# Decay rows issued from ScalarE, and token rows multiplied in two column groups after the value products

## The chip, the cores and the metric

The kernel runs on one core of one Trainium2 chip. The metric is the device time of one execution in microseconds; the kernel before takes 475.36 us (median of three runs, 474.98 to 475.89). The diagnosis rests on one profiled execution, which took 474.5 us.

## What is computed

Two blocks follow each other. The first is a recurrent gated linear attention over 4 batches, 8 heads, 768 tokens and a head dimension of 48. The second is a mixture of experts (8 experts, one per token, width 1024) over the resulting 3072 rows of 384.

```python
state = np.zeros((B, H, D, D))
for t in range(S):
    state = alpha[:, :, t, :, None] * state + np.einsum('bhd,bhde->bhde', k[:, :, t], v[:, :, t])
    y[:, :, t] = np.einsum('bhd,bhde->bhe', q[:, :, t], state)
x = y.transpose(0, 2, 1, 3).reshape(B * S, H * D)
logits = x @ w_gate
expert_idx = np.argmax(logits, axis=1)          # one expert per token
gate_w = softmax(logits)[expert_idx]
out = gate_w * (relu(x @ w1[expert]) @ w2[expert])
```

## The kernel before

**Tiling.** The tokens of a batch are cut into six chunks of 128. A *step* `s` is one chunk of one batch: chunk `c = s // 4`, batch `b = s % 4`, 24 steps in all. Within a chunk the recurrence is written as matrix products: with the cumulative product of the decays (`cp`, and its inverse `icp`), keys are multiplied by `icp` and queries by `cp` (`operands`, GpSimd), both are transposed on TensorE (`transposes`), their products give the scores (`scores`), which are masked (`mask`, VectorE, two tiles dA and dB) and multiplied with the values (`attend`). From the second chunk on, `read_state` adds the carried state, scaled by the decay over the chunk boundary (`scale_state`, the tile U). `keys_values` forms the state's increment. All three write one PSUM tile, `y`. Then `result` copies the outputs to SBUF as `yT` (ScalarE), `add_state` forms the new state (VectorE, the tile acc), `rows` turns `yT` into rows and router logits with one product per pair of heads (TensorE, the tile `x`), `logits` and `gate` make the router's weight (VectorE and ScalarE), and `keep_rows` writes the weighted rows `xs` to memory for the second block.

**Order of the work.** The order is written out by hand: a loop over `i` from -4 to 24 issues scores of step `i`, result and state of step `i-1`, transposes of `i+1`, operands of `i+2` and the exponentials of step `i+5` (lines 454 to 490). Each engine works through its own instructions in that order; waits between engines are put in by the framework. So on ScalarE an iteration runs: yT (line 367), logarithms (244), the copy of the keys kT (304), two exponentials (253, 254), the router's exponential gex (400), xs (408). On VectorE it runs: acc (375, 377), the masks dA and dB (319), the copy of the queries qT (302), at a chunk's end the decay rows er (269, 270), then lgn and lmin (393, 394) and gw (401, 402). On TensorE it runs: scores (311), at a chunk's start the turning of the decay rows ep (281), transposes (299), cum (250), x (383), the state's reading (338), attend (348), keys and values (359).

**The decay over a chunk boundary.** For each step one row of `cp` (the last) and one of `icp` (the first) are copied by DMA into a small tile `dec` (line 262). Once per chunk, `decay_rows` multiplies them with one row of alpha (the tile alpha0, loaded at line 264) into er, TensorE turns er into columns (`decay_cols`, ep), and VectorE copies these as E, which `scale_state` needs. ep and cum share one PSUM tile.

**SyncE's queue.** SyncE issues, in the loop's order, all loads of alpha, k, q and v (line 236, two steps at a time, some three iterations ahead), the decay rows (262), the alpha row (264), the weighted rows (409, which waits for xs), and from `i = 4` the first expert's weights (185, 188). ScalarE issues two small loads at the start and none in the loop.

**The second block.** After the loop a ranking of tokens (lines 498 to 622) is followed by gathers, the experts' products on TensorE and scatters (from line 829 on). None of it is touched; its first instruction waits for the last logits.

```python
            do(rows, i - 1)
            for s in sums[1:]:
                cums(s)
            do(read_state, i)
            do(attend, i)
            do(keys_values, i)
            do(logits, i - 1)
```

Of the kernel before, what the change touches and what calls it, by code (L numbers as in the profile page):

```python
# [18 lines left out]
def kernel(  # L19
# [26 lines left out]
    nc = tc.nc  # L46
    B, H, S, D = q.shape
    C = 128
    NB = S // C
# [4 lines left out]
    E = moe_w_gate.shape[1]  # L54
# [3 lines left out]
    D2 = 2 * D  # L58
    DP = 64
    HC = C // 2  # L60
# [18 lines left out]
    iw = consts.tile([C, NP, D2 + E], F32)  # L79
    alpha0 = consts.tile([B, NB, H, D], F32)  # L80
# [10 lines left out]
    def second_consts():  # L91
        nc.vector.tensor_scalar_mul(iw[:, :, D2:], iw[:, :, D2:], -1.0)
        for i in range(2):
            nc.vector.tensor_copy(
                iw[i * DP : (i + 1) * DP, :, i * D : (i + 1) * D],
                ident[i * DP : (i + 1) * DP, None, i * DP : i * DP + D].to_broadcast([DP, NP, D]),
            )
# [21 lines left out]
    def late_consts(i):  # L119
        if i == 0:  # L120
            nc.gpsimd.memset(lt_strict[:], 1.0)
            nc.gpsimd.affine_select(
                lt_strict[:], lt_strict[:], compare_op=ALU.is_gt, fill=0.0,
                base=0, pattern=[[1, C]], channel_multiplier=-1,
            )
            nc.gpsimd.memset(ones_sq[:], 1.0)
        if i == 1:
            nc.gpsimd.memset(zero_e[:], 0.0)
            nc.gpsimd.memset(keep[:], 1.0)
            nc.gpsimd.memset(keep[:, :, 0:1], 0.0)  # L130
        if i in (2, 3):
            for ti, tf, pattern, base, mult in list(iotas.values())[3 * (i - 2) : 3 * (i - 1)]:
                nc.gpsimd.iota(ti[:], pattern=pattern, base=base, channel_multiplier=mult)
                nc.gpsimd.tensor_copy(tf[:], ti[:])
            if i == 2:

                nc.gpsimd.memset(key0[:, 0:1], float(16 * N))
        if i == 4:

            nc.gpsimd.tensor_copy(iota_r[:], iota_f[:])  # L140
            nc.gpsimd.tensor_scalar(
                tok_n[:], tokv[:, NT // 2 :], scalar1=-1.0, scalar2=float(N // 2), op0=ALU.mult, op1=ALU.add,
            )
            nc.gpsimd.tensor_copy(tokv[:, NT // 2 :], tok_n[:])
# [33 lines left out]
    def fetch_part(g, i):  # L178

        if i == 0:  # L180
            g["w1"] = wpool.tile([C, DB, F], F32, name="w1")
            g["w2"] = wpool.tile([C, FB, Dm], F32, name="w2")
        if i < 6:
            a, h = i // 2, i % 2
            nc.sync.dma_start(g["w1"][:, a, h * F // 2 : (h + 1) * F // 2], moe_w1[0, a * C : (a + 1) * C, h * F // 2 : (h + 1) * F // 2])
        else:
            f = 2 * (i - 6)
            nc.sync.dma_start(
                g["w2"][:, f : f + 2], moe_w2[0, f * C : (f + 2) * C, :].rearrange("(a p) d -> p a d", p=C),
            )  # L190
# [24 lines left out]
    def cb(s):  # L215
        return s // B, s % B

    with tc.tile_pool(name="ld", bufs=6) as ld, \
# [6 lines left out]
        decay = {}  # L225
# [16 lines left out]
        def logs(s):  # L242
            t = work.tile([C, Dm], F32, name="lna", bufs=4)
            nc.scalar.activation(t[:], st[s]["a"].rearrange("s h d -> s (h d)"), AF.Ln)
            st[s]["lna"] = t

        def cums(s):
            c, b = cb(s)
            cum = ps.tile([C, 512], F32, name="cum")
            nc.tensor.matmul(cum[:, :Dm], lhsT=cum_m[:], rhs=st[s]["lna"][:], start=True, stop=True)  # L250
            cp = work.tile([C, Dm], F32, name="cp", bufs=6)
            icp = work.tile([C, Dm], F32, name="icp", bufs=6)
            nc.scalar.activation(icp[:], cum[:, :Dm], AF.Exp, scale=-1.0)
            nc.scalar.activation(cp[:], cum[:, :Dm], AF.Exp)
            st[s]["cp"], st[s]["icp"] = cp, icp


            for cc, i, row in ((c, 1, icp[0:1, :]), (c + 1, 0, cp[C - 1 :, :])):
                if 0 < cc < NB:
                    if cc not in decay:  # L260
                        decay[cc] = work.tile([B, 2, Dm], F32, name="dec", bufs=3)
                    nc.sync.dma_start(decay[cc][b : b + 1, i, :], row)
                if i and b == 0 and c:
                    nc.sync.dma_start(alpha0[:, c], alpha[:, :, c * C, :])

        def decay_rows(c):
            t = by_half(er[:B])
            d = decay[c].rearrange("b i (a p d) -> b i a p d", a=2, p=NP)
            nc.vector.tensor_tensor(t, d[:, 0], d[:, 1], op=ALU.mult)
            nc.vector.tensor_tensor(t, t, alpha0[:, c].rearrange("b (a p) d -> b a p d", a=2), op=ALU.mult)  # L270
# [7 lines left out]
        def decay_cols(c):  # L278
            ep = ps.tile([C, NP, C], F32, name="ep", tag="cum")
            for p in range(NP):  # L280
                nc.tensor.transpose(ep[:, p, :], pair(er[:], p), ident[:])
            decay[c] = work.tile([C, NP, B], F32, name="E", bufs=2)
            nc.vector.tensor_copy(decay[c][:], ep[:, :, :B])  # L283
# [95 lines left out]
        def rows(s):  # L379
            d = st[s]  # L380
            d["x"] = ps.tile([C, NP, C], F32, name="x")
            for m in range(NP):
                nc.tensor.matmul(  # L383
                    d["x"][:, m, : D2 + E], lhsT=d["yT"][:, m // 2, m % 2, :], rhs=iw[:, m, :], start=True, stop=True,
                )

        def at_row(s):
            c, b = cb(s)
# [23 lines left out]
        def do(f, i, *a):  # L412
            if 0 <= i < NT:
                f(i, *a)
# [7 lines left out]
        def new_sums(i):  # L422
            return range(sums_to(i - 1) + 1, sums_to(i) + 1)
# [10 lines left out]
        def loads_for(i):  # L434
            loads(("a", sums_to(i + 1)), ("v", i), ("k", i + 2), ("q", i + 2))

        def idle(n):

            t = ps.tile([C, NP, C], F32, name="sA")
            for _ in range(n):  # L440
                nc.tensor.matmul(t[:, :2, :], lhsT=er[:, 0].rearrange("s a d -> s (a d)"), rhs=er[:, :2], start=True, stop=True)
# [12 lines left out]
        for i in range(-4, NT + 1):  # L454
            loads_for(i + 3)
            do(scores, i)
            do(result, i - 1)
            do(add_state, i - 1)
            for s in new_sums(i + 1):
                logs(s)  # L460
            if 0 < i < NT and i % B == 0:
                decay_cols(i // B)
            do(mask, i, 0)
            do(mask, i, 1)
            if -2 < i < 0:
                idle(3)
            do(transposes, i + 1)
            sums = list(new_sums(i))
            for s in sums[:1]:
                cums(s)  # L470
            do(operands, i + 2)
            do(scale_state, i)
            if 0 < i + 1 < NT and (i + 1) % B == 0:
                decay_rows((i + 1) // B)
            do(rows, i - 1)
            for s in sums[1:]:
                cums(s)
            do(read_state, i)
            do(attend, i)
            do(keys_values, i)  # L480
            do(logits, i - 1)
            do(gate, i - 1)
            do(keep_rows, i - 1)
            if i == -3:
                second_consts()
            late_consts(i - 1)
            if 4 <= i < 14:
                fetch_part(groups[0], i - 4)
            if 15 <= i < 23:
                next(first_sums)  # L490
# [168 lines left out]
    def chain(g, terms, out, res):  # L659
# [44 lines left out]
        return p1, p2, p7, p6, p5, c22, p34  # L704

    def layer1(g, rows, ahead):
        n, m = g["n"], g["n"] // 2
        h0, h1 = slice(0, m), slice(m, n)
# [41 lines left out]
        for a in range(FH):  # L750
            p1, p2, p7, p6, p5, c22, p34 = tile_parts(a)
            p1()
            p2()
            p7()
            p6()
            if prev:
                prev()
            next(rows, None)
            p5()
            c22()  # L760
            prev = p34
# [175 lines left out]
```

## Time and profile before

| | |
|---|---|
| median of three runs | 475.36 us |
| the profiled execution | 474.5 us |
| its span on the core | 472.7 us |
| TensorE busy | 415.8 us (88%) |
| VectorE, ScalarE, GpSimd busy | 233.3, 171.8, 139.6 us |
| first block, to 171.5 us: TensorE busy | 147 us |
| ranking, 171.5 to 195 us: TensorE busy | 5.2 us |
| experts, from 195 us: TensorE busy | 263.7 us |
| DMA share, 69.7 to 125 us | 0.90, at 188 to 201 GB/s |
| granted clock of TensorE, 96.4 to 125 us | 0.88 |

A line of the timeline gives the start in us, the length in us, the engine, the source line, the operation, its output and inputs, shapes, and in brackets how long the engine was idle before it and which event ended that. PE is TensorE, PEld its loading of weights, DVE VectorE, ACT ScalarE, POOL GpSimd, SPq the queue of SyncE. A 32-bit product appears as two matmul instructions. Instructions in a row of one kind are merged ("x8").

### The profile page before, as it was taken

To read this page: it belongs to the slowest core of one execution; us is meant where nothing else is said; L and a number is where in the kernel's file an instruction comes from. 1 tells how busy PE (TensorE), PEld (TensorE's weight loads), DVE (VectorE), ACT (ScalarE), POOL (GpSimd) and SP (SyncE) were. 2 spreads that over 40 slices of the span, in tenths; PEclk is the share of its full clock that TensorE was granted. 3 is DMA by queue.
4 is the path that set the end of the run, shared out by engine and by line. 5 is a ranking of instruction groups with operands and counts; after the bars stand their busy time and mean duration, and the time that the engine had idled before them with its cause. 6 is when DMAs were issued, how large, how long until landed. Compare 5 with 4: busy or idle time off the path is not lost.

```text
span 472.7 us, 8960 instructions
## 1 busy us (share of the span) xinstructions
PE 415.8 (88%) x3356; PEld 362.7 (77%) x3356; DVE 233.3 (49%) x640; ACT 171.8 (36%) x454; POOL 139.6 (30%) x169
## 2 busy tenths in 40 slices
PE   7893979979799921699999999999999999999991
PEld 5683878868688811597997997997997988979970
DVE  3343534445556568347446447357257365473500
ACT  4652636446353410041352251251350431523511
POOL 3442432424567405710024024022041140200102
PEclk9997998979999965599999999999999999999997
DMA  9986788989862107414235225315414432400001
GB/s 178 203 175 129 162 198 177 185 197 218 185 138 68 53 33 266 123 41 133 61 124 190 91 96 187 128 57 187 150 44 174 168 118 91 172 2 17 31 0 49
DMA packets 119969, 59.05 MB, mean 125 GB/s; under 512 B 102806, under 2 KB 114159, under 8 KB 119924
## 3 DMA queue, kind: packets, MB, share of 16 engines
q1 hardware_dynamic: 116084, 48.86, 40.1%
q0 software_dynamic: 3424, 9.59, 5.8%
q8 instruction: 27, 0.44, 0.4%
q14 instruction: 18, 0.15, 0.1%
q10 hardware_dynamic: 416, 0.01, 0.0%
HBM read 48.95 MB, written 9.58 MB: 124 GB/s over the span
## 4 chain that ended last, share of the span: by engine, by line
PE 58%; issue 5%; DVE 4%; POOL 2%; ACT 1%; DMA 1%; POOLq 0%; ACTq 0%; DVEq 0%
PE pA L727 12%; PE pB L727 9%; PE pA L783 8%; PE pC L798 8%; PE pC L727 5%; PE pB L783 4%; PE pC L783 2%; PE tp L645 2%; PE sA L311 2%; PE y L348 1%; PE x L383 1%; PE tp L828 1%; PE tp L299 1%; PE y L338 1%; DVE xgT L646 1%
## 5 line engine op out<-in xcount | busy, mean ns | idle before, releaser
L815 POOL DMA_INDIRECT out_dram<-zo,s_idx x29 | 31.8, 1096 | 208.0 <-ACT zo L814 114.3
L671 ACT COPY u<-pA 128x212 f32<-128x212 f32 (+7 forms) x80 | 25.5, 318 | 83.5 <-PE pA L783 70.1
L173 DVE TENSOR_TENSOR h_sb<-pB,u 128x212 f32<-128x212 f32 (+7 forms) x64 | 23.1, 361 | 65.8 <-PE pB L727 49.2
L798 PE MATMUL pC<-h_sb,w 128*128 128x424 f32 (+7 forms) x128 | 43.9, 496 | 0.0
L289 POOL TENSOR_TENSOR kqb<-k_sb,icp 128x384 f32<-128x384 f32 x24 | 24.1, 1004 | 62.4 <-ACT xs L408 30.0
L798 PEld LDWEIGHTS pC<-h_sb,w 128*128 128x128 f32 x128 | 24.1, 190 | 16.0 <-issue 6.7
L727 PE MATMUL pA<-t,s 128*128 128x212 f32 (+7 forms) x128 | 33.2, 341 | 1.0 <-ACT u L671 0.4
L635 POOL DMA_INDIRECT xg<-x_rows,g_idx x29 | 30.0, 1033 | 10.7 <-issue 6.7
L727 PE MATMUL pA<-xgT,w 128*128 128x212 f32 (+7 forms) x128 | 32.5, 335 | 0.0
L383 PEld LDWEIGHTS x<-iw,yT 128*128 128x128 f32 x192 | 25.6, 197 | 6.9 <-ACT yT L367 1.4
L299 PE MATMUL tp<-ident,kqb 128*128 128x128 f32 x192 | 28.6, 294 | 1.3 <-POOL kqb L289 1.3
L176 DVE TENSOR_TENSOR th<-h_sb,th 128x212 f32<-128x212 f32 (+7 forms) x64 | 23.1, 361 | 10.5 <-ACT h_sb L740 10.5
L311 PE MATMUL sA<-qT,kT 48*128 48x128 f32 x192 | 27.7, 285 | 0.2 <-ACT kT L304 0.2
L671 ACT COPY p<-pA 128x212 f32<-128x212 f32 (+7 forms) x40 | 13.1, 328 | 40.4 <-DVE t L176 25.8
L311 PE MATMUL sB<-qT,kT 48*128 48x128 f32 x192 | 27.7, 285 | 0.0
L727 PE MATMUL pC<-xgT,w 128*128 128x212 f32 (+7 forms) x128 | 27.4, 338 | 0.0
L727 PE MATMUL pB<-t,w 128*128 128x212 f32 (+7 forms) x128 | 27.0, 333 | 0.0
L383 PE MATMUL x<-iw,yT 128*128 128x104 f32 x192 | 25.9, 280 | 1.1 <-ACT yT L367 1.1
L299 PEld LDWEIGHTS tp<-ident,kqb 128*128 128x128 f32 x192 | 22.7, 149 | 4.4 <-POOL kqb L289 2.3
L740 ACT ACTIVATE h_sb<-h_sb 128x424 f32<-128x424 f32 (+7 forms) x32 | 17.1, 533 | 24.0 <-DVE h_sb L173 24.0
L289 POOL TENSOR_TENSOR kqb<-q_sb,cp 128x384 f32<-128x384 f32 x24 | 24.9, 1035 | 2.3 <-DMA q_sb<-in_q_dram 2.3
L250 PE MATMUL cum<-lna,cum_m 128*128 128x384 f32 x48 | 21.7, 536 | 3.8 <-DVE E L283 2.5
(176 smaller groups left out, 930.7 us busy)
## 6 DMA issues: line engine op xcount, KB each, us to landing
w<-in_moe_w_dram SPq DMA_DIRECT2D x14, 1536.0 KB, 6.8
x_rows<-xs SPq DMA_DIRECT2D x24, 192.0 KB, 2.1
a_sb<-in_alpha_dram SPq DMA_DIRECT2D x11, 384.0 KB, 4.9
k_sb<-in_k_dram SPq DMA_DIRECT2D x11, 384.0 KB, 5.5
q_sb<-in_q_dram SPq DMA_DIRECT2D x11, 384.0 KB, 5.2
v_sb<-in_v_dram SPq DMA_DIRECT2D x11, 384.0 KB, 5.6
w<-in_moe_w_dram SPq DMA_DIRECT2D x6, 256.0 KB, 3.4
w<-in_moe_w_dram SPq DMA_DIRECT2D x4, 384.0 KB, 3.5
```

Source lines behind the costliest of these rows:

```text
L173: eng.tensor_tensor(out, a, b, op=ALU.add)
L176: eng.tensor_tensor(out, a, b, op=ALU.subtract)
L289: nc.gpsimd.tensor_tensor(by_half(kq[:, i]), d[n].rearrange("s (a p) d -> s a p d", a=2), d[e][:].rearrange("s (a p d) -> s a p d", a=2, p ...
L299: nc.tensor.transpose(tp[:, p, :], pair(kqb[s % 3][:, i], p), ident[:])
L311: nc.tensor.matmul(t[:, p, :], lhsT=d["kT"][r : r + D, p, :], rhs=d["qT"][r : r + D, p, :], start=True, stop=True,)
L383: nc.tensor.matmul(d["x"][:, m, : D2 + E], lhsT=d["yT"][:, m // 2, m % 2, :], rhs=iw[:, m, :], start=True, stop=True,)
L635: nc.gpsimd.indirect_dma_start(out=g["xg"][:r, j, :], out_offset=None, in_=x_d[:, :], in_offset=bass.IndirectOffsetOnAxis(ap=g["gi"](j, r) ...
L671: nc.scalar.copy(t[:, :m], bank["A"][:, :m])
L727: nc.tensor.matmul(out, lhsT=ops[n_][0], rhs=ops[n_][1], start=first and n_ == names[0], stop=True, skip_group_check=True,)
L783: nc.tensor.matmul(out, lhsT=lhs, rhs=rhs, start=first and f == 0, stop=True, skip_group_check=True)
L798: nc.tensor.matmul(d2[:, :n], lhsT=w2[:, f, 2 * C :], rhs=h[:, f, :n], start=(f == 0), stop=(f == FB - 1),)
L815: ins = nc.gpsimd.indirect_dma_start(out=out[:, :], out_offset=bass.IndirectOffsetOnAxis(ap=g["si"](j, r), axis=0), in_=zo[:r], in_offset= ...
```

## The change

The two decay rows of a step are issued by ScalarE, in its order right behind the two exponentials that make them. The row of alpha for a chunk boundary is loaded one chunk earlier. The product `rows` of step `i-1` moves from before the state's reading to behind `keys_values` of step `i`, just ahead of the logits that use it; the second exponentials of the first iterations come behind `attend`. And each of its four products is cut into two of 64 tokens, which write partitions 0 to 63 and 64 to 127 of the same PSUM tile.

```diff
-                    nc.sync.dma_start(decay[cc][b : b + 1, i, :], row)
-                if i and b == 0 and c:
-                    nc.sync.dma_start(alpha0[:, c], alpha[:, :, c * C, :])
+                    nc.scalar.dma_start(decay[cc][b : b + 1, i, :], row)
+            if b == 0 and c + 1 < NB:
+                nc.sync.dma_start(alpha0[:, c + 1], alpha[:, :, (c + 1) * C, :])
...
-                nc.tensor.matmul(
-                    d["x"][:, m, : D2 + E], lhsT=d["yT"][:, m // 2, m % 2, :], rhs=iw[:, m, :], start=True, stop=True,
-                )
+                for o in (0, HC):
+                    nc.tensor.matmul(
+                        d["x"][o : o + HC, m, : D2 + E], lhsT=d["yT"][:, m // 2, m % 2, o : o + HC], rhs=iw[:, m, :],
+                        start=True, stop=True,
+                    )
...
-            do(rows, i - 1)
+            do(read_state, i)
+            do(attend, i)
             for s in sums[1:]:
                 cums(s)
-            do(read_state, i)
-            do(attend, i)
             do(keys_values, i)
+            do(rows, i - 1)
             do(logits, i - 1)
```

## The prediction

> **What bounds the kernel now.** I read the page first (busy shares, chain), then who waited for whom, then the timeline of one quiet iteration of the loop and of one at a chunk's end, and last SyncE's queue. The expert block (from 195 us, TensorE busy 263.7 of 277 us) is not touched, and its way in hangs on the last logits, so whatever the loop gains or loses passes to the end one for one. In the loop two waits stand out (us in total, times, longest):
>
> ```profile
> DVE er L269 <- DMA dec<-icp: 20.0, 4, 8.7
> PE ep L281 <- DVE lgn L393: 13.6, 4, 7.4
> ```
>
> VectorE waits for decay rows, and TensorE then waits for VectorE. Between these stalls TensorE sets the pace. A quiet iteration:
>
> ```profile
> 85.11 1.03 PE L383 MATMUL x<-iw,yT 128*128 128x104 f32 x8
> 86.08 0.66 PE L338 MATMUL y<-qT,U 48*48 48x128 f32 x16
> 86.19 0.19 DVE L393 TENSOR_REDUCE lgn<-x 128x8 f32<-128x32 f32 x1 [0.66 <-PE x L383]
> ...
> 86.66 0.64 PE L348 MATMUL y<-dA,v_sb 128*48 128x128 f32 x8
> 87.14 0.61 PE L348 MATMUL y<-dB,v_sb 128*48 128x128 f32 x8
> 87.58 0.53 PE L359 MATMUL y<-v_sb,kqb 128*48 128x48 f32 x16
> 87.62 0.58 ACT L408 ACTIVATE xs<-x,gw 128x384 f32<-128x384 f32 x1 [0.56 <-DVE gw L402]
> 88.03 0.37 PE L311 MATMUL sA<-qT,kT 48*128 48x128 f32 x1
> 88.20 0.58 ACT L367 COPY yT<-y 128x512 f32<-128x512 f32 x1
> 88.89 0.36 DVE L377 TENSOR_TENSOR acc<-y,U 128x192 f32<-128x192 f32 x1 [1.45 <-ACT yT L367]
> 89.22 0.69 DVE L319 TENSOR_TENSOR dA<-sA,cmask 128x512 f32<-128x512 f32 x1
> 89.83 0.68 DVE L319 TENSOR_TENSOR dB<-sB,cmask 128x512 f32<-128x512 f32 x1
> ```
>
> TensorE goes from kind to kind without a hole; the first scores of the iteration before start at 82.45, so the period is 88.03 - 82.45 = 5.58 us. See also the order on ScalarE: xs of step i-1 stands ahead of yT of step i, and acc and the masks wait behind yT. At a chunk's end:
>
> ```profile
> 92.05 0.50 SPq L262 DMA_DIRECT2D dec<-icp  x1
> ...
> 94.60 0.65 DVE L269 TENSOR_TENSOR er<-dec 4x384 f32<-4x384 f32 x1 [3.49 <-DMA dec<-icp]
> 95.28 1.23 DVE L270 TENSOR_TENSOR er<-er,alpha 4x384 f32<-4x384 f32 x1
> 96.44 0.17 DVE L393 TENSOR_REDUCE lgn<-x 128x8 f32<-128x32 f32 x1
> ...
> 99.01 0.36 DVE L377 TENSOR_TENSOR acc<-y,U 128x192 f32<-128x192 f32 x1 [1.33 <-ACT yT L367]
> 99.28 0.16 DVE L283 COPY E<-ep 128x16 f32<-128x16 f32 x1
> ```
>
> The products that lgn needs were long done; lgn stood behind er, and er behind a DMA. From lgn to lgn these five iterations take 15.7, 10.8, 10.25, 10.25 and 6.7 us: 25.8 us over five times 5.58. The two iterations behind the third, at a lower clock (6.41 and 6.29 us against 5.27 and 5.58), cost 1.9 us more.
>
> **Edit 1, rows issued by ScalarE.** It takes 40 issues off SyncE, which stands ahead of the rows with loads:
>
> ```profile
> 87.17 3.05 SPq L262 DMA_DIRECT2D dec<-icp  x1
> ```
>
> On SP an icp row took 0.50 to 3.05 us to issue, a cp row mostly 0.54. ScalarE has the chunk's last rows at the end of the exponentials two iterations ahead of er's turn (sum below), so er no longer waits, if they land within 6.7 us; the slowest in the trace (issued 64.65, er at 68.69) took 4.0. The new wait is ScalarE's, for its own exponentials; behind it stand gex and xs, and behind them VectorE's gw, acc and masks. The only ScalarE issues in the trace:
>
> ```profile
> 1.27 0.93 ACTq L448 DMA_DIRECT2D iw<-in_moe_w_gate_dram  x2
> ```
>
> That is 0.46 us each, 0.9 a step. The bound above is SP's dearest pair, 3.05 + 0.54 = 3.6 us. I take 1.0, nearer to ScalarE's own row. The Trainium skill ("DMA: Bandwidth & Descriptors", Issuing engines are not separate DMA queues) speaks against a gain: transfers of all issuers share the same 16 engines, and another issuer saves only issue time. Taken so, rows would still need up to the 4.0 us; that is inside 6.7, so the sum is the same by both. The alpha row, a chunk earlier on SP (0.73 us), costs nothing: SP gains more than it spends.
>
> **Edit 2, rows behind the value products.** TensorE's work hardly changes. Eight instructions took 0.97 us with the change of tile shape (85.11 to 86.08), 0.87 of it theirs. Now there are sixteen in pairs on two column groups. Nearest row: attend, same shape, sixteen in 0.92 us (86.66 to 87.58) at 128 columns, 0.115 a pair; at 104 columns 0.093 a pair, 0.75 us. The skill ("TensorEngine Tiling (Array Packing)", Restrictions) says that column groups lose the fast weight load. If loading bound it, the row of L359 tells the price: sixteen 48-column loads and products in 0.45 us; scaled to 64 columns 0.60, under 0.75. Bounds 0.60 and 0.92; I take 0.75. The number of changes of tile shape stays four per iteration.
>
> What counts is that rows now end the iteration on TensorE, and that a ring closes: attend, keys_values, rows, lgn, gex, gw, xs, yT, acc, dA, dB, next attend. Before, lgn came 1.84 us ahead of the next scores and this hid. The ring, from the start of rows:
> - to lgn: 0.75 + 0.21 (86.19 less 85.11 less 0.87) = 0.96
> - lgn to acc: 96.44 to 99.01 = 2.57 (the same at 69.74 to 72.31)
> - acc to dA 0.33, dA to dB 0.61
> - dB to the second half of attend: 0.68 and a handover of 0.10 (er to ep 0.14, E to cum 0.05) = 0.78
> - second half of attend 0.44, keys_values 0.45
>
> Sum 6.14 us, against TensorE's 5.58 - 0.97 + 0.75 = 5.36. So the quiet iteration gets 0.56 longer, and TensorE idles 0.8 in it. At the end, without cum, it ran at 4.6 us and will also take 6.14.
>
> Inside the ring: cp ends 4.2 us after lgn (yT 1.9, lna, kT and both exponentials behind it), the next gex is due 6.14 + 0.48 = 6.6 after it. The two issues (1.0) fit into these 2.4 us. er is ready for its turn at 4.75 and takes 1.1 (two of 0.55 where GpSimd is idle, as at 41.5), before the next lgn at 6.14: hidden too. In the iteration behind a chunk's end, E (acc + 0.27 + 0.16) holds cum, and cum (0.64) the state's reading: acc at 3.53, E done 3.96, cum 4.01 to 4.65, reading 4.75, attend 5.33 to 6.25, rows at 6.70. So 0.56 more, five times.
>
> **The sum.** Iterations 0 and 1: attend 1 waits for dB (18.87 + 0.78), the second cum for cp (20.82), so keys_values end and rows of step 0 start at 22.1 (before 19.74). Then 22 periods: 7.2 and 6.4 for the two iterations with a second cum (6.14 + 0.7 and 0.35 or 0.25 of issuing not hidden; the second 0.25 alone), 15 x 6.14 = 92.1, 5 x 6.70 = 33.5; together 139.2, so rows of step 22 start at 161.3. The last: lgn at 162.25, yT 1.89 + 0.58 later, rows of step 23 at 164.8, lgn 165.8. It was 168.28: 2.5 us earlier. In short, about 26 us of stalls are given back and some 23 are spent on a longer ring and a later start. The profiled execution would go from a span of 472.7 to 470.2 and from 474.5 to 472.0 us; the median lies 0.86 above that execution, so 475.36 - 2.5 = 472.9 us.
>
> **Rivals.**
> - *Longer ring* (0.17): rows at 0.92 and handovers at 0.14 make it 6.35; 22 x 0.21 = 4.6, so 477.5. For it: no pair of 64 x 104 is in the trace.
> - *ScalarE issues wait as SP's do* (0.13). Place: between cp and gex. From 2.4 us a pair on, each microsecond enters the ring. SP's icp rows behind a load averaged 1.8, with 0.54 just within; at 3.0 a pair it costs 0.6 x 19 = 11.4, less the 2.5: 484. Against it: ScalarE's queue holds no loads of its own.
> - *The rows still come late* (0.05): a landing over 6.7 us keeps half of the four later stalls, some 10 us: 483. Or loads fall behind: a pair of steps, 2.55 MB each 12.3 us, asks for 207 GB/s where stages reached 188 to 204; k has some 6 us of slack (0.05), 477.
> - *No ring* (0.05): VectorE and ScalarE pass the chain in less than 5.36 us; TensorE's pace then gives 23 x 5.36 + 5 x 1 and ends near 457. Against it: the 2.57 us from lgn to acc stands in two places.
>
> **How the numbers follow.** About 0.2% (1 us) is what a measurement of this kernel can tell from no change. The ring as summed has 0.55: 468 to 475.5, of it 0.45 faster, 0.08 same and 0.02 slower; with "no ring" faster is 0.50. "Longer ring" gives 0.06 to same. So 0.50, 0.14, 0.36. The range 467 to 481 leaves out "no ring", most of the issue rival and the late rows; its size comes from 22 rings times the bounds of rows (-3.3, +3.7 us) and of the handovers (1 us).
>
> **What would show it.** Right: no wait of er for dec over 1 us; lgn to lgn near 6.1 everywhere, 6.7 behind a chunk's end; acc waiting for yT and attend for dB; ScalarE's issues near 0.5 us. Wrong: a period of 5.4 (no ring), gex waiting for an issue, k arriving late, or TensorE's clock under 0.9 because it now idles in every iteration.

## The result, and the profile after

The changed kernel takes 467.38 us (median of four runs, 466.32 to 468.48), against 475.4 us for the kernel before in the same session (four runs): a ratio of 0.983, 95% interval 0.981 to 0.986. It is faster by 8 us. The forecast was 472.9 with a range from 467 to 481; so the direction held, the time lies at the lower edge of the range, and the gain is about three times the 2.5 us expected.

The profiled execution took 467.84 us, with a span of 466.0. First the waits of the changed kernel (us in total, times, longest):

```profile
ACT gex L402 <- DVE lmin L396: 54.5, 23, 4.0
...
DVE lgn L395 <- PE x L384: 35.8, 24, 3.5
...
DVE acc L377 <- ACT yT L367: 19.9, 16, 1.3
```

The wait of er for decay rows, 20.0 us before, is gone from the list: nothing is left of it. The three waits shown were there before too, in the kernel before:

```profile
ACT gex L400 <- DVE lmin L394: 42.3, 22, 10.0
...
DVE acc L377 <- ACT yT L367: 23.4, 16, 2.2
...
DVE lgn L393 <- PE x L383: 11.0, 14, 2.5
```

What is new is that lgn waits for rows in all 24 steps, 35.8 us in total instead of 11.0, and that gex waits longer behind it, though the long stalls are gone. The waits alone don't show a ring; a quiet iteration does:

```profile
78.02 0.90 PE L384 MATMUL x<-iw,yT 128*64 128x104 f32 x16
...
78.97 0.19 DVE L395 TENSOR_REDUCE lgn<-x 128x8 f32<-128x32 f32 x1 [1.24 <-PE x L384]
...
79.39 0.30 ACT L402 ACTIVATE gex<-lgn,lmin 128x8 f32<-128x8 f32 x1 [2.24 <-DVE lmin L396]
...
80.26 0.58 ACT L410 ACTIVATE xs<-x,gw 128x384 f32<-128x384 f32 x1 [0.48 <-DVE gw L404]
80.74 0.58 ACT L367 COPY yT<-y 128x512 f32<-128x512 f32 x1
...
81.42 0.36 DVE L377 TENSOR_TENSOR acc<-y,U 128x192 f32<-128x192 f32 x1 [1.25 <-ACT yT L367]
...
82.29 0.68 DVE L319 TENSOR_TENSOR dB<-sB,cmask 128x512 f32<-128x512 f32 x1
...
83.03 0.65 PE L348 MATMUL y<-dB,v_sb 128*48 128x128 f32 x8
...
83.50 0.53 PE L359 MATMUL y<-v_sb,kqb 128*48 128x48 f32 x16
...
83.86 0.90 PE L384 MATMUL x<-iw,yT 128*64 128x104 f32 x16
```

Read it as a chain from rows to rows. Each line starts about when the line above it ends (the recorded times of neighbours overlap by up to 0.2 us), or a handover later: the products of rows, lgn behind them, gex behind lgn and lmin, gw (two small instructions, left out) ahead of xs, yT behind xs on ScalarE, acc behind yT, the masks behind acc on VectorE (dA, left out, at 81.69), the second half of attend behind dB, keys_values, and rows again. From 78.02 to 83.86 it takes 5.84 us; lgn comes every 5.83 us in all twelve quiet periods. Between these steps there are only handovers. This is the ring that the prediction described, a little shorter.

Where the loop's time went, by the start of lgn in the timelines of both kernels. The last column is the first experiment, told below.

| lgn to lgn, us | before | after | edit 1 alone |
|---|---|---|---|
| start of the first | 20.81 | 23.37 | 21.34 |
| 1st period | 6.03 | 6.81 | 6.69 |
| 2nd and 3rd (the first chunk's end) | 20.95 | 13.06 | 12.35 |
| 4th to 19th | 104.62 | 95.72 | 90.74 |
| 20th to 23rd | 15.87 | 20.60 | 15.89 |
| start of the last | 168.28 | 159.56 | 147.01 |
| from there to the end of the span | 304.4 | 306.4 | 305.3 |

The stretch with the stalls gives 16.8 us back (20.95 + 104.62 - 13.06 - 95.72). The start and the tail of the loop take 8.1 us of that away. What follows the loop took 2 us more in this execution, though the code there is the same; it took 305.3 us with edit 1 alone. Why it varies by one or two us isn't settled.

### The profile page after: what moved, and what is told of

Same layout as the page of the kernel before. It is cut to its first block, busy times and chain, and to the rows that moved or that the text cites. A ratio compares the mean times of both kernels' runs of the same rounds, so it can differ in the third digit from the quotient of the medians.

```text
span 466.0 us, 9245 instructions
## 1 busy us (share of the span) xinstructions
PE 410.4 (88%) x3548; PEld 350.4 (75%) x3548; DVE 229.8 (49%) x640; ACT 167.7 (36%) x454; POOL 140.2 (30%) x169
## 4 chain that ended last, share of the span: by engine, by line
PE 57%; issue 7%; DVE 5%; ACT 3%; POOL 2%; DMA 1%; POOLq 0%; ACTq 0%; DVEq 0%
PE pA L729 12%; PE pB L729 9%; PE pA L785 8%; PE pC L800 8%; PE pC L729 5%; PE pB L785 4%; PE pC L785 2%; PE y L348 2%; PE x L384 2%; PE tp L647 2%; PE tp L830 1%; PE y L338 1%; ACT xs L410 1%; ACT yT L367 1%; PE sA L311 1%
## 5 line engine op out<-in xcount | busy, mean ns | idle before, releaser
L289 POOL TENSOR_TENSOR kqb<-k_sb,icp 128x384 f32<-128x384 f32 x24 | 25.5, 1062 | 60.6 <-PE y L359 23.2
L311 PE MATMUL sA<-qT,kT 48*128 48x128 f32 x192 | 27.7, 284 | 0.2 <-DVE qT L302 0.2
L311 PE MATMUL sB<-qT,kT 48*128 48x128 f32 x192 | 27.7, 285 | 0.0
L402 ACT ACTIVATE gex<-lgn,lmin 128x8 f32<-128x8 f32 x24 | 7.2, 301 | 56.7 <-DVE lmin L396 54.5
L299 PE MATMUL tp<-ident,kqb 128*128 128x128 f32 x192 | 26.4, 279 | 1.2 <-POOL kqb L289 1.2
L311 PEld LDWEIGHTS sA<-qT,kT 48*128 48x128 f32 x192 | 23.1, 187 | 3.8 <-ACT kT L304 0.8
L384 PE MATMUL x<-iw,yT 128*64 128x104 f32 x384 | 23.0, 265 | 2.9 <-ACT yT L367 2.9
L785 PE MATMUL pA<-th,s 128*128 128x212 f32 (+7 forms) x128 | 24.6, 335 | 0.5 <-ACT u L673 0.5
L729 PEld LDWEIGHTS pA<-t,s 128*128 128x128 f32 x128 | 21.2, 190 | 4.9 <-ACT u L673 3.4
```

The lines of the kernel that those rows point to most:

```text
L289: nc.gpsimd.tensor_tensor(by_half(kq[:, i]), d[n].rearrange("s (a p) d -> s a p d", a=2), d[e][:].rearrange("s (a p d) -> s a p d", a=2, p ...
L299: nc.tensor.transpose(tp[:, p, :], pair(kqb[s % 3][:, i], p), ident[:])
L311: nc.tensor.matmul(t[:, p, :], lhsT=d["kT"][r : r + D, p, :], rhs=d["qT"][r : r + D, p, :], start=True, stop=True,)
L384: nc.tensor.matmul(d["x"][o : o + HC, m, : D2 + E], lhsT=d["yT"][:, m // 2, m % 2, o : o + HC], rhs=iw[:, m, :], start=True, stop=True,)
L729: nc.tensor.matmul(out, lhsT=ops[n_][0], rhs=ops[n_][1], start=first and n_ == names[0], stop=True, skip_group_check=True,)
L785: nc.tensor.matmul(out, lhsT=lhs, rhs=rhs, start=first and f == 0, stop=True, skip_group_check=True)
```

## The experiments

The theory put to the test: edit 1 (ScalarE issues the rows) ends the stalls and is the whole gain; edit 2 (rows behind keys_values) closes the ring and costs time in every iteration. The main rival: the two edits need each other, or the stalls end because rows moved out of the way. Three more questions follow from that: what the column groups do, whether the ring really sets the period, and whether it can be opened. Times are medians with 95% intervals of the ratio to the kernel before on the same chip; the quiet period is lgn to lgn away from a chunk's end, and "last lgn" is the start of the last lgn in us. The runs come from several chips, so ratios are to be compared, and times only roughly.

| kernel | us | ratio | interval | quiet period | last lgn |
|---|---|---|---|---|---|
| the change | 467.38 | 0.983 | 0.981 to 0.986 | 5.83 | 159.56 |
| edit 1 alone | 454.10 | 0.955 | 0.950 to 0.960 | 5.58 | 147.01 |
| edit 2 alone | 482.84 | 1.017 | 1.011 to 1.023 | 5.97 | 174.52 |
| change, rows at full width | 474.60 | 0.998 | 0.995 to 1.000 | 6.16 | 168.42 |
| edit 1 and column groups | 453.16 | 0.955 | 0.951 to 0.959 | 5.58 | 147.26 |
| change, two more VectorE steps | 475.37 | 1.003 | 1.001 to 1.005 | 6.20 | 167.48 |
| edit 1 alone, the same two steps | 456.20 | 0.962 | 0.959 to 0.966 | 5.58 | 149.75 |
| ring opened, first try | 487.11 | 1.025 | 1.019 to 1.031 | 6.95 | 178.11 |
| ring opened, second try | 458.66 | 0.965 | 0.959 to 0.972 | 5.44 | 153.44 |
| second try, more buffers | 454.09 | 0.954 | 0.950 to 0.958 | 5.44 | 148.67 |
| edit 1 alone, those buffers | 454.84 | 0.956 | 0.952 to 0.960 | 5.58 | 146.73 |
| edit 1 without the alpha row | 455.51 | 0.958 | 0.954 to 0.962 | 5.58 | 147.50 |

**Edit 1 alone.** The kernel before with the first hunk of the diff only.

```diff
-                    nc.sync.dma_start(decay[cc][b : b + 1, i, :], row)
-                if i and b == 0 and c:
-                    nc.sync.dma_start(alpha0[:, c], alpha[:, :, c * C, :])
+                    nc.scalar.dma_start(decay[cc][b : b + 1, i, :], row)
+            if b == 0 and c + 1 < NB:
+                nc.sync.dma_start(alpha0[:, c + 1], alpha[:, :, (c + 1) * C, :])
```

> Edit 1 alone (decay rows on ScalarE, alpha row a chunk earlier); rows stay at full width in their old place. My theory: the five late er were the stall and rows behind the value products only make a ring that is longer than TensorE's own period. Then no er waits over 1 us, the quiet period stays 5.58 us, 26 + 1.9 us come back less some 0.5 us a chunk's end: about 450 us, faster than the whole change (467.4). Rival 'loads bound': two steps ask for 2.55 MB in 11.2 us, 228 GB/s; at the 215 to 220 reached after the change the first dozen iterations take 5.9 us: 455 to 460, with GpSimd waiting for k. Rival 'the move is needed': ScalarE's two issues (1.0 us) now stand between cp and a gex that is due 0.4 us later, and the delay passes to acc, masks and attend: periods near 6.2, 465 or more.

Measured: 454.10 us, 13 us under the full change, and some 4 us over what was expected; the part on the sizes below tells why. Its timeline in an iteration at a chunk's end:

```profile
74.33 0.19 DVE L393 TENSOR_REDUCE lgn<-x 128x8 f32<-128x32 f32 x1 [0.50 <-PE x L383]
...
79.34 0.54 DVE L269 TENSOR_TENSOR er<-dec 4x384 f32<-4x384 f32 x1
...
80.38 0.17 DVE L393 TENSOR_REDUCE lgn<-x 128x8 f32<-128x32 f32 x1
```

er has no bracket: VectorE came to it straight from its own work, and the rows lay there. From lgn to lgn it is 6.05 us, where it was 10.25. The quiet period keeps its 5.58: the ring isn't there, since lgn's products come ahead of the state's reading. In most quiet iterations gex stands behind the two issues here, 0.90 us behind lgn instead of 0.48, and the period stays: the rival that the move is needed falls. So the gain is all edit 1's, and edit 2 takes some 60% of it away.

**Edit 2 alone.** The full change with the issues back where they were.

```diff
-                    nc.scalar.dma_start(decay[cc][b : b + 1, i, :], row)
-            if b == 0 and c + 1 < NB:
-                nc.sync.dma_start(alpha0[:, c + 1], alpha[:, :, (c + 1) * C, :])
+                    nc.sync.dma_start(decay[cc][b : b + 1, i, :], row)
+                if i and b == 0 and c:
+                    nc.sync.dma_start(alpha0[:, c], alpha[:, :, c * C, :])
```

> Edit 2 alone (rows behind the value products in two column groups); decay rows and alpha row on SyncE as before. My theory: period 5.83 us as after the change, and the waits of er for late rows come back on top, less the 1.1 us or so that the longer ring hides: 4 to 6 us at the first chunk's end, 2 to 3 at the next three: 478 to 485 us, slower than before. Rival 'the longer ring hides late rows': er waits under 1 us except for the first, 468 to 472.

Measured: 482.84 us, slower than the kernel before. Of the waits of this kernel, the one of er for its rows:

```profile
DVE er L269 <- DMA dec<-icp: 9.4, 2, 6.7
```

The longer period hides part of the stalls (9.4 us here, and 3.2 us more in front of an er that the view puts down to another DMA; 20.0 before), but doesn't end them. The rival that moving rows ends the stalls falls. The two edits don't add up plainly: edit 2 adds 6.2 us to last lgn without edit 1 (174.52 against 168.28) and 12.6 us with it, which fits a stall that is there anyway and hides a longer iteration.

**Rows at full width.** The full change with rows as one product of 128 tokens per pair of heads.

```diff
-                for o in (0, HC):
-                    nc.tensor.matmul(
-                        d["x"][o : o + HC, m, : D2 + E], lhsT=d["yT"][:, m // 2, m % 2, o : o + HC], rhs=iw[:, m, :],
-                        start=True, stop=True,
-                    )
+                nc.tensor.matmul(
+                    d["x"][:, m, : D2 + E], lhsT=d["yT"][:, m // 2, m % 2, :], rhs=iw[:, m, :], start=True, stop=True,
+                )
```

> The whole change, but the four products of rows keep their 128 tokens. My theory: TensorE's piece of the ring grows from 0.75 to 0.87 us and a change of tile shape of 0.1 us comes in, so the period is 5.83 + 0.2 = 6.0 us: 20 periods, +4 us, 471. Rival 'column groups bring nothing': 467 to 468. Rival 'they bring most': 475 or more.

Measured: 474.60 us, where 471 was expected: the column groups bring 1.5% where rows is in the ring. In the timeline of this kernel:

```profile
80.97 0.53 PE L359 MATMUL y<-v_sb,kqb 128*48 128x48 f32 x16
...
81.42 1.14 PE L383 MATMUL x<-iw,yT 128*128 128x104 f32 x8
...
82.60 0.19 DVE L393 TENSOR_REDUCE lgn<-x 128x8 f32<-128x32 f32 x1 [1.57 <-PE x L383]
```

From keys_values to rows it is 0.45 us (0.36 with groups), from rows to lgn 1.18 (0.95 with groups): together 0.32, and the period is 0.33 longer. Without the groups edit 2 would have used up the whole gain of edit 1: the interval of 0.998 reaches to 1.

**Edit 1 and column groups.** Edit 1 alone plus the groups, rows in its old place (the diff just shown, reversed).

> Edit 1 and the column groups alone: rows split in two groups of 64 tokens, but in the old place between cum and the state's reading. My theory: here no ring binds, TensorE's sum does; sixteen instructions take 0.73 in place of 0.87 us, but one more change of tile shape (128x128 to 128x64 to 64x64) costs about 0.1: 5.55 us a period, 453 to 454.5, no difference from edit 1 alone (454.1). Rival 'column groups pay by themselves': 5.4 us, 450. Rival 'they cost': 457 or more.

Measured: 453.16 us, no difference from edit 1 alone. The same edit is worth 1.5% inside the ring and nothing outside it, where the period stays 5.58.

**Two more VectorE steps, in the ring and outside it.** Two multiplications by 1.0 (plus 0.0) on gw, right ahead of xs: once in the full change, once in edit 1 alone. The output stays what it was.

```diff
             nc.vector.reciprocal(d["gw"][:], d["gw"][:])
+            for _ in range(2):
+                nc.vector.tensor_scalar(d["gw"][:], d["gw"][:], scalar1=1.0, scalar2=0.0, op0=ALU.mult, op1=ALU.add)
```

> The whole change with two small VectorE multiplications of the router weight by 1.0 behind the reciprocal, each 0.19 us by the spacing of gw's two instructions; the output is the same. They lie in the ring. My theory: the period grows from 5.83 by 0.38 to 6.2 us, 22 rings, +8 us: 475. Rival 'TensorE or the loads set the period after the change too': 467 to 468.

> The same two VectorE multiplications in edit 1 alone, where rows stand early and the same chain has an iteration more to run. My theory: the period stays 5.58, a few tenths at each chunk's end: 454 to 456. Rival 'VectorE's work as such sets the pace': +8 us, 462.

Measured: with the ring 475.37 us, and the period grows from 5.83 to 6.20 us. Without it 456.20 us at an unchanged quiet period of 5.58. The two steps in the timeline of the first:

```profile
83.74 0.34 DVE L406 TENSOR_SCALAR gw<-gw 128x1 f32<-128x1 f32 x2
...
84.18 0.58 ACT L412 ACTIVATE xs<-x,gw 128x384 f32<-128x384 f32 x1 [0.85 <-PE tp L299]
```

They take 0.34 us, or 0.38 with the handover, and last lgn comes 7.9 us later, a third of a us per step. That 0.34 us on an engine that is idle half the time costs 2% is the plainest sign that the ring sets the period. (The bracket at xs names TensorE's tp, but xs needs gw: the two releasers ended close together, and the view names one.) With edit 1 alone last lgn comes 2.7 us later; it arises at the start, at some chunk ends and in the last iterations, none of it in the quiet ones.

**The ring opened, first try.** The full change with logits of the step before moved behind the masks, and gate and xs behind the exponentials, an iteration later.

```diff
             do(mask, i, 1)
+            do(logits, i - 2)
...
+            do(gate, i - 2)
+            do(keep_rows, i - 2)
             do(read_state, i)
...
-            do(logits, i - 1)
-            do(gate, i - 1)
-            do(keep_rows, i - 1)
```

> The whole change, but logits of step i-2 come behind the masks of step i, and its gate and weighted rows behind the exponentials, one iteration later than now: VectorE and ScalarE no longer hold acc, masks and yT of the next step behind them, so the ring is open. My theory: the period falls to TensorE's own 5.4 us; lgn of the last step comes some 16 us earlier, 451 us. Rival 'loads bound': 238 GB/s would be asked, so the first dozen iterations stay near 5.9 and only the rest gains: 460 to 463. Rival 'no ring': no change, 467.

Measured: 487.11 us, a miss. The quiet period is 6.95 us, so a new and longer ring was closed. One turn of it in the timeline:

```profile
82.86 0.30 ACT L402 ACTIVATE gex<-lgn,lmin 128x8 f32<-128x8 f32 x1 [0.84 <-ACT cp L254]
...
83.67 0.58 ACT L410 ACTIVATE xs<-x,gw 128x384 f32<-128x384 f32 x1 [0.42 <-DVE gw L404]
...
84.31 0.94 PE L384 MATMUL x<-iw,yT 128*64 128x104 f32 x16 [1.30 <-ACT xs L410]
```

TensorE waits 1.30 us at rows for xs of the step before, which must read the one PSUM tile x first. xs stood behind gex, and gex behind the exponentials and their two issues on ScalarE; those wait for this iteration's cum.

**The ring opened, second try.** logits and gex at once behind yT, gw's two instructions behind the masks, xs behind the copy of the keys.

```diff
             do(result, i - 1)
+            do(logits, i - 2)
+            do(gate, i - 2)
...
             do(mask, i, 1)
+            do(gate_end, i - 2)
...
             do(transposes, i + 1)
+            do(keep_rows, i - 2)
...
-            do(logits, i - 1)
-            do(gate, i - 1)
-            do(keep_rows, i - 1)
```

> The whole change with the ring opened again, this time with short ways: logits and the gate's exponential of step i-2 right behind yT of step i-1, its weight gw behind the masks, its weighted rows behind the copy of the keys. In the first try (487 us) the exponential and the weighted rows stood behind the two exponentials and their DMA issues, and rows of the next step waited for the weighted rows to leave the one tile x: a new ring of 6.95 us. By my reckoning from the traces ScalarE is now done with x 1.2 us before rows needs it. My theory: TensorE's own period, 5.58 - 0.97 + 0.73 = 5.35 us, and 450 us, some 4 under edit 1 alone. Rival 'loads bound' (238 GB/s asked, 220 seen): 453 to 458 with GpSimd waiting for k. Rival 'another ring': over 460.

Measured: 458.66 us. The quiet period falls to 5.44 us, but the kernel stays behind edit 1 alone, for another wait:

```profile
102.25 0.47 SPq L414 DMA_DIRECT2D x_rows<-xs  x1
...
105.47 0.58 ACT L413 ACTIVATE xs<-x,gw 128x384 f32<-128x384 f32 x1 [4.05 <-DMA x_rows<-xs]
```

xs has two buffers, and the DMA that empties one stands in SyncE's queue among the loads. xs now comes on its buffer before that: 12.3 us of waiting in five iterations, which ScalarE passes on to rows (here 2.27 us of idle TensorE) and yT.

**The second try with more buffers, and its control.** Four buffers for xs; to make room, cp and icp get five in place of six. The control gives the same buffers to edit 1 alone.

```diff
-            cp = work.tile([C, Dm], F32, name="cp", bufs=6)
-            icp = work.tile([C, Dm], F32, name="icp", bufs=6)
+            cp = work.tile([C, Dm], F32, name="cp", bufs=5)
+            icp = work.tile([C, Dm], F32, name="icp", bufs=5)
...
-            xs = work.tile([C, NP, D2], F32, name="xs")
+            xs = work.tile([C, NP, D2], F32, name="xs", bufs=4)
```

> The second opening of the ring (logits and the router's exponential right behind yT, the gate behind the masks, xs behind kT) with four buffers for xs instead of two; to make room, cp and icp have five instead of six. Theory (the ring is open, and what kept that kernel at 0.965 was xs waiting for its buffer, whose x_rows DMA stood behind loads on SyncE): no wait of xs for x_rows over 1 us, 5.44 us per quiet iteration all along, ratio 0.945 to 0.955 (448 to 453 us), so level with edit 1 alone or a little under it. Rival (the loads of k and v, or the fewer cp buffers, take the place of that wait): 0.958 to 0.968, with waits for k or of ScalarE for cp of 3 us and more.

> Edit 1 alone with the same buffers (xs four, cp and icp five). Theory: nothing waits for these buffers in that order, so no difference from edit 1 alone: ratio 0.9545 within 0.004, 5.58 us per quiet iteration. Rival (the buffers matter in the old order too): beyond that, and then the kernel with the open ring is to be read against this one.

Measured: 454.09 and 454.84 us. The wait of xs for x_rows is gone, so it was the buffer. But at a quiet period of 5.44 the kernel is only level with edit 1 alone: two periods around chunk ends still take 6.9 and 7.6 us, and its last lgn is later than in edit 1 alone (148.67 against 147.01), as logits come an iteration later. Part of the 7.6 us is a late load: GpSimd waits 4.4 us for k up to 105.9 us, U then starts at 108.1, and the state's reading waits 1.67 us for it. An open ring makes the harm of edit 2 good; no kernel tried here gets under edit 1 alone by more than its interval.

**Edit 1 without the alpha row.** The kernel before with only the two decay rows issued by ScalarE.

```diff
-                    nc.sync.dma_start(decay[cc][b : b + 1, i, :], row)
+                    nc.scalar.dma_start(decay[cc][b : b + 1, i, :], row)
```

> The kernel before with nothing but the two decay rows issued by ScalarE; the alpha row stays where it was, behind the first step of a chunk's exponentials. Theory (the alpha row was never the late one, as it is asked for three steps ahead of the last decay rows): as edit 1 alone, ratio 0.9545 within 0.004. Rival (the alpha row behind loads takes the place of the decay rows): er waits for alpha at some chunk's end by over 1 us, ratio 0.96 or more.

Measured: 455.51 us, a ratio of 0.958 whose interval overlaps that of edit 1 alone. The first er of this kernel, its second half:

```profile
35.63 0.64 DVE L270 TENSOR_TENSOR er<-er,alpha 4x384 f32<-4x384 f32 x1 [0.96 <-DMA alpha<-in_alpha_dram]
```

At the first chunk's end the alpha row is late by 0.96 us, where the expectation had it never late; at the four others there is no such wait. By the timeline the earlier load is worth up to 1 us, too little for these times to tell.

## Why the prediction was right on the mechanism and off on the sizes

**The stalls** were read rightly: er waited for rows, the rows stood behind loads in SyncE's queue, and issuing them elsewhere ends all four waits. The size was wrong: 25.8 + 1.9 = 27.7 us were put down as given back (about 26 in the summary), and edit 1 alone gave 21.3 (last lgn 168.28 to 147.01). The sum took five lgn-to-lgn periods over 5.58 each. The fifth of these, 6.66 us, was no stall: er does not wait there, and the same period takes 6.65 us with edit 1 alone. That is 1.1 us too much. And er stands ahead of lgn: it delays one lgn and not the next, so the period behind a stall is too short (4.72 to 5.27 us in four of five). Taken in pairs, stalled period and the one behind it, the kernel before has 80.2 us in five pairs and edit 1 alone 58.4. That is 21.8 back, of which the low clock is a part; ten periods of 5.58 are 55.8, so 2.6 us of the chunk ends' own work stay. Another 0.7 us comes back in the period after the third pair, which ran at the low clock before (6.29 us, now 5.59), and the start costs edit 1 1.2 us: together the 21.3.

**ScalarE's issues** were priced at 1.0 us a step and hidden. Both hold in the quiet iterations. This is the view of the decay rows' tile, before and after (duration of an issue in ns: least, median, most):

```profile
L262 SPq DMA_DIRECT2D dec<-cp x20: 525/539/2166, 16.5 to 120.2; - x20
L262 SPq DMA_DIRECT2D dec<-icp x20: 502/1000/3051, 33.4 to 140.7; - x20
```

```profile
L262 ACTq DMA_DIRECT2D dec<-cp x20: 504/547/1669, 7.4 to 101.5; - x20
L262 ACTq DMA_DIRECT2D dec<-icp x20: 504/505/556, 20.3 to 124.6; - x20
...
DMA to landing us min/median/max: 2.0/3.8/5.0
```

The pair costs 1.05 us, and from the third iteration on gex is held up by lmin, not by an issue. In the second an issue of 1.20 us stands in the way, and gex comes 1.21 us behind lgn instead of 0.42; the prediction had counted on some issuing that would not be hidden there. The first icp row leaves at 20.3 us where it left at 33.4. In one iteration, at 67.72, the timeline names a decay row's DMA as what ended gex's idle time; gex comes 0.42 us behind lgn there as in the others, so it isn't a cost.

**The skill's rule on issuers** (Trainium skill, "DMA: Bandwidth & Descriptors", Issuing engines are not separate DMA queues) said that another issuer saves only issue time. The runs agree on the transfer: a row took 2.0 to 5.0 us to land, median 3.8, no faster than from SyncE (1.6 to 5.1, median 2.6; the 4.0 that the prediction called the slowest was not). The gain is the place in the order, not the transfer; the bound of 6.7 us that the prediction set against the landing was never reached.

**The ring** is the one predicted, and "no ring" was rightly held unlikely. Each edge, predicted and measured in the iteration shown: rows to lgn 0.96 and 0.95, lgn to acc 2.57 and 2.45, acc to dA 0.33 and 0.27, dA to dB 0.61 and 0.60, dB to the second half of attend 0.78 and 0.74, that half 0.44 and 0.47, keys_values 0.45 and 0.36. The sum is 5.84 instead of 6.14. No edge was far off, but nearly all the small excesses have one sign. The runs tell where two of them come from. keys_values to rows is 0.45 at full width, as predicted, and 0.36 with the column groups. lgn to acc is 2.59 in edit 2 alone, as predicted, and 2.45 in the full change and at full width: it got shorter with edit 1, by an effect told at the end. 0.06 more is in acc to dA. The 0.33 stands in the quiet iterations of the kernel before, where the last scores end 0.03 us ahead of dA; in the change they end at 80.01, long before acc, and it is 0.27. That fits a dA that waited for scores before, which are no part of the ring. What the column groups lose in loading weights, which the prediction weighed, can't be read apart: the edge that it belongs to, rows to lgn, came out as summed.

**The sum**, by its own terms, at the last lgn (165.8 predicted, 159.56 measured). Twelve quiet periods at 5.83 instead of 6.14: -3.7. The five behind a chunk's end, 32.2 instead of 33.5: -1.3. The three of the tail, 16.1 instead of 18.4: -2.35. The last one: +1.0. The start: +0.1. The step that failed as an argument is "At the end, without cum, it ran at 4.6 us and will also take 6.14." In the last four steps there is no keys_values and no acc either, so the ring is shorter:

```profile
151.70 0.66 PE L338 MATMUL y<-qT,U 48*48 48x128 f32 x16 [1.58 <-ACT yT L367]
...
152.76 0.85 PE L348 MATMUL y<-dB,v_sb 128*48 128x128 f32 x8
...
153.39 1.61 PE L384 MATMUL x<-iw,yT 128*64 128x104 f32 x16
```

rows follows attend directly; two of the tail's periods take 5.06 us. The third takes 5.96, with the clock down; in edit 2 alone, with the clock up, all three take 5.06. The other terms are sizes. The prediction bounded the ring at 0.2 us below its sum (22 rings, -3.3 us for rows and -1 us for handovers); it came out 0.3 below, as keys_values and the edges through ScalarE had been given no bound. That is why the time lies at the edge of the range. On the side of cost, the 23 us "spent on a longer ring and a later start" measure 12.6 (last lgn 147.01 to 159.56): 2.0 at the start, 5.8 in the 1st to 19th periods and 4.7 in the tail. Both halves of the balance were too large, the 26 by 5 us and the 23 by 10, and the difference of two large terms carries the error of both. That the forecast said faster was in part luck: with the stalls at their real 21.3 us and the cost as it was summed, it would have said slower by some 2 us (21.3 less 23).

**The rivals.** "Longer ring" is refuted (5.83, not 6.35), and so is "ScalarE issues wait": the median pair takes 1.05 us, and even the slowest two issues, 0.56 and 1.67, would stay under 2.4. Rows are never late. Loads do not fall behind more than they did: GpSimd waits for k 7.3 us in the changed kernel and 10.6 before. "No ring" falls with the quiet period of 5.83, and with the two VectorE steps that lengthen it.

## What to carry to other kernels

Judge the edits of one change apart: the first was worth 4.5%, the second took more than half of that back, and together they looked like a modest success. Before moving an operation later on the busiest engine, follow its result through the other engines back to that engine's next turn; if the way round is longer than the engine's own work, every small step on it, 0.3 us on an idle engine, sets the pace. And size a stall by the stretch up to where the order has recovered, not by the one long period.

## What the runs showed of the hardware

**Small holes left TensorE's clock alone; longer ones lowered it in some places and not in others.** The page's row of the granted clock, in 40 slices, of the kernel before (11.8 us each) and of the changed kernel (11.65 us each):

```profile
PEclk9997998979999965599999999999999999999997
```

```profile
PEclk9999999999999555899999999999999999999997
```

The prediction feared a clock under 0.9 from idling in every iteration. In the quiet iteration shown TensorE is busy for 5.59 of 5.83 us, and the clock is 1.00 from 23 to 150 us. The first try at opening the ring went further: TensorE waits 1.30 us in every 6.95, and the clock is 1.00 from 84 to 119.5 us. Before, where TensorE waited 1.9 to 7.4 us at the stalls, three slices of the loop stood at 7 or 8. Length alone doesn't decide it: after a wait of 1.88 us, up to 96.7, the clock was 0.50 from 97.5 to 101.3 us; after one of 1.87 us, up to 125.2, it was 1.00 to 129. At the end of the changed kernel's loop, with waits of 1.6 and 2.9 us, the clock from 151 to 162 us was 0.59, and the same sixteen instructions of rows took nearly twice the time:

```profile
157.86 1.65 PE L384 MATMUL x<-iw,yT 128*64 128x104 f32 x16 [2.87 <-ACT yT L367]
```

1.65 us against 0.90 is most of the +1.0 us of the last period above. The Trainium skill ("TensorE: Matmul & The Clock Gate", Part 1) has it that the clock follows how busy TensorE has lately been. These rows fit that, and add that 1.3 us of idling in 7 was not enough to lose it here.

**ScalarE took up its work sooner where no semaphore instruction stood ahead of it.** In a quiet iteration of edit 2 alone lgn to gex takes 0.48 us and the reciprocal of gw to xs 0.33; in the full change 0.42 and 0.25. Nothing else in these edges differs: together 0.14 us, which is the whole difference of the two quiet periods (5.97 and 5.83), and the kernel at full width has the short ones too. It looks as if ScalarE were quicker for issuing DMAs, but the views of gex's line, in edit 2 alone and in the full change, point elsewhere:

```profile
L402 ACTq EVENT_SEMAPHORE  x22: 17/17/17, 42.8 to 174.9; - x22
```

```profile
L402 ACTq EVENT_SEMAPHORE  x5: 17/17/17, 139.4 to 160.0; - x5
```

EVENT_SEMAPHORE, 17 ns here, is an instruction of ScalarE's sequencer. In edit 2 alone it stands ahead of all but the first two gex, and those two come 0.42 us behind lgn, though ScalarE issues nothing in that loop. In the full change it stands ahead of only the last five gex, and these come 0.48 behind; from the third to the nineteenth it is 0.42. So the short handover goes with the missing instruction, and not with an issue as such. Why it is missing where decay rows are issued from ScalarE was not tried.

**The column groups shorten more than the product.** Sixteen products of 64 x 104 in two groups took 0.90 us from first start to modelled end, eight of 128 x 104 in the same place 1.14. Behind keys_values, the start came 0.09 us earlier as well; the trace doesn't tell why.
